# Mamba2 scan and ELU feed-forward on one core: whole-half decays with their sums on GpSimd, low words on ScalarE, and an earlier last weight piece

## The chip, the cores and the metric

The kernel runs on one core of a Trainium2 chip. The core has five engines that each work through their own queue in order: PE (TensorE, matrix products), DVE (VectorE), ACT (ScalarE), POOL (GpSimd) and SP (SyncE, which here only issues DMAs). An instruction whose inputs or buffers aren't ready holds up what stands behind it on its engine. The metric is the device time of one execution in microseconds (us).

## What is computed

Inputs are `x` (4 batches, 8 heads, 768 tokens, 32 wide), decays `a`, and `B` and `C` (16 wide). First a chunked scan, then a feed-forward layer on the 3072 rows that the scan gives:

```python
cum = np.cumsum(log_a, axis=-1)                       # within a chunk of 32
L = np.exp(cum[:, :, :, None] - cum[:, :, None, :]) * causal
y_intra = einsum('bhij,bhjd->bhid', einsum('bhin,bhjn->bhij', Cc, Bc) * L, xc)
y_inter = einsum('bhin,bhnd->bhid', Cc, state) * exp(cum)
state = exp(sum(la)) * state + sum_j(Bc * xc * exp(cum[-1] - cum))
...
h = x @ w_in                                          # (3072, 256) by (256, 2048)
g = np.where(h > 0.0, h, np.exp(np.minimum(h, 0.0)) - 1.0)
out = g @ w_out                                       # (2048, 256)
```

The weights arrive as 64-bit floating-point numbers, and the kernel makes 32-bit ones of their words itself.

## The kernel before

The 3072 tokens are 12 blocks (n = 0 to 11) of 256 tokens. The kernel scans in chunks of 64 tokens instead of 32. For a block the scan has these parts: the table of decays `L` (128 x 8 heads x 2 x 64), the scores `C B`, the product of the two (`weigh`, DVE, L550), the sums for the states (`sums`, PE, L571), the states (`states`: DVE at L588, then a masked copy `Sx` on POOL at L593), the products with the start states (`across`, L616) and inside the chunk (`inside`, L634), whose results ACT copies into `yT` (L651). The feed-forward part has a first product (`l1`, L667, later `l1_words`, L787), the ELU (`elu`: two ACT steps, L680 and L687, and one DVE step, L689, which frees the PSUM buffer of the product) and a second product (`l2`, L829).

**Decays of a block.** `spread_cum(n)` (L377) issues two DMAs that spread the running sums of the logarithms over the partitions into `L`. For one head, `decay_of` (L518) runs two exps on ACT over 128x64 (L521), in place, with `bias=ncum[:, u, row:row + 1]`: the exp subtracts the sum at this partition's token while it reads. After every fourth head, two `affine_select` on POOL (L526, 64x512 each) set to zero what lies after the diagonal. `ncum` is made by PE and a DVE step (L369) just ahead of the loop described next.

**Weights.** There are 16 pieces of 128x512 numbers, 0 to 7 of `w_in` and 8 to 15 of `w_out`. For piece `i`, `w_take` (L966) takes a magnitude on ACT (`w_abs`, L196), the low word (`w_low`, on ACT at L205 or on DVE at L209) and the sign on DVE (L223); `w_give` (L972) makes the high word in two DVE steps (L231, L238) and adds the low word on POOL (`w_sum`, L248). PE can use the piece after that sum.

**Order of the work around the change.** The order is written out by hand. A first loop (L1092) has 12 steps s = 0 to 11. Step s does `l1` for one of (1, 0), (1, 1), (1, 2), (0, 4), (1, 3), (0, 5), (1, 4), (0, 6), (1, 5), (0, 7), (1, 6), (1, 7), where (n, i) is block n with piece i; the first eight steps each do one head of the decays of block 2; odd steps take and give one piece of weights (5 to 10); the ELU follows one step behind. After step 7 come `scores(2)` and `sums(2)`; in step 8 `states(2)`; in step 9 half of the decays of block 3; in step 10 `across(2)` and `inside(.., 2)`. A second loop (L1173) has steps j = 0 to 7: `l2(0, j)`, `l1` of block 2 or 3, pieces 11 to 15 in steps 0, 2, 3, 4 and 5, the rest of block 3's decays in step 0, and `decay` of blocks 4 and 5 in `scan_ahead`. In step 4 `words_of_y(2)` (L750) splits the result of the scan into two words: `y1` (one half on ACT, L755, one on DVE, L759, but both on ACT for n = 4) and `y0` (DVE, L762); `both_of_y` (DVE, L772) follows in step 5. `words_of_w` (ACT L736, DVE L737) and `low_of_w` (POOL, `sub`, L845) split pieces of `w_in`.

From j = 8 on, `l1_words(n, m)` makes the first product in three passes of PE: `y1` by the high word, `y0` with the low word `w0`, and `both_y` with `both_w`. Their order is chosen at L786:

```python
for ps, lhs, rhs in passes if n > 2 and m == 0 else passes[2:] + passes[:2]:
```

So the pass with `both_y` comes first except at the first product of the blocks from 4 on. PSUM has seven buffers for all of this and an eighth for the second product; a new product waits for the last reader of the buffer it takes.

Of the kernel before, what the change touches and what calls it, by code (L numbers as in the profile page):

```python
# [14 lines left out]
ALU = mybir.AluOpType  # L15
ACT = mybir.ActivationFunctionType

P = 128
Q = 64
# [13 lines left out]
def kernel(  # L33
# [27 lines left out]
    nc = tc.nc  # L61
    NB, NH, S, D = x.shape
    N = B.shape[-1]
    NG = S // BLK
# [18 lines left out]
    def psum(shape, name):  # L83
        return p_a.tile(shape, F32, tag="a", name=name)
# [7 lines left out]
    for k in range(4):  # L92
        (nc.scalar if k % 2 else nc.sync).dma_start(
            out=la0[BH * k:BH * (k + 1)],
            in_=a.rearrange("b h (c s) -> (b h) c s", s=P)[:, 0:2, :])
# [5 lines left out]
    st = {}  # L101

    def place(n):

        return 2 * (n // (2 * NG)) + n % 2, n // 2 % NG

    def rows_of(n):
        b, g = place(n)
        return slice(NG * NH * b + g, NG * NH * (b + 1), NG)
# [93 lines left out]
    def w_low(i, eng, cols=slice(None)):  # L203
        if eng is nc.scalar:
            eng.activation(  # L205
                pieces[i][0][:, :, cols], w_words(i)[0][:, :, cols], ACT.Identity,
                scale=2.0 ** -51, bias=two)
        else:
            eng.tensor_scalar(  # L209
                out=pieces[i][0], in0=w_words(i)[0], scalar1=2.0 ** -51, scalar2=2.0,  # L210
                op0=ALU.mult, op1=ALU.add)
# [30 lines left out]
    def w_high(i):  # L242
        w_high_a(i)
        w_high_b(i)
# [34 lines left out]
    for v in range(2):  # L279
        nc.gpsimd.affine_select(  # L280
            out=low16[Q * v:Q * v + Q], in_=low16[Q * v:Q * v + Q], pattern=[[1, Q]],
            compare_op=ALU.is_ge, fill=-65536.0, base=0, channel_multiplier=-1)
# [4 lines left out]
        out=hmask, in_=hmask, pattern=[[-N, NH]], compare_op=ALU.is_ge, fill=0.0,  # L287
        base=0, channel_multiplier=1)
    nc.gpsimd.affine_select(
        out=hmask, in_=hmask, pattern=[[N, NH]], compare_op=ALU.is_ge, fill=0.0,  # L290
        base=N - 1, channel_multiplier=-1)
# [7 lines left out]
        out=minus, in0=ident, scalar1=-1.0, scalar2=None, op0=ALU.mult)  # L299
# [213 lines left out]
    def decay(n, q):  # L513

        decay_of(n, 2 * q)
        decay_of(n, 2 * q + 1)

    def decay_of(n, h):  # L518
        L, row = st[n]["L"], rows_of(n).start + NG * h
        for u in range(2):  # L520
            nc.scalar.activation(  # L521
                L[:, h, u], L[:, h, u], ACT.Exp, bias=ncum[:, u, row:row + 1])
        if h % 4 == 3:
            for v in range(2):
                part = L[Q * v:Q * v + Q, h - 3:h + 1]
                nc.gpsimd.affine_select(  # L526
                    out=part, in_=part, pattern=[[0, 4], [0, 2], [1, Q]],
                    compare_op=ALU.is_ge, fill=0.0, base=0, channel_multiplier=-1)

# [218 lines left out]
    def words_of_y(n):  # L750

        y = yT[n // 2].rearrange("p k b u i -> p k (b u i)")
        y1 = conv.tile([P, KC, 2 * BLK], F32R, tag="y1", name="y1", bufs=1)
        y0 = conv.tile([P, KC, 2 * BLK], F32R, tag="y0", name="y0", bufs=1)
        nc.scalar.activation(y1[:, 1], y[:, 1], ACT.Copy, scale=NEAR / WORD)  # L755
        if n == 4:
            nc.scalar.activation(y1[:, 0], y[:, 0], ACT.Copy, scale=NEAR / WORD)
        else:
            nc.vector.tensor_scalar(  # L759
                out=y1[:, 0], in0=y[:, 0], scalar1=NEAR / WORD, scalar2=None, op0=ALU.mult)  # L760
        for k in range(KC):
            nc.vector.scalar_tensor_tensor(  # L762
                out=y0[:, k], in0=y1[:, k].bitcast(F32), scalar=WORD, in1=y[:, k],
                op0=ALU.mult, op1=ALU.subtract)
        y_words[n] = y1, y0
# [11 lines left out]
    def l1_words(n, m, between=None):  # L777

        cols = slice(m % 2 * P, (m % 2 + 1) * P)
        w, w0 = k_words[m // 2]  # L780
        w1, both_w, w0 = w[:, 0, :, cols], w[:, 1, :, cols], w0[:, :, cols]
        y1, y0, both_y = y_words[n]
        high, both = psum([P, 2 * BLK], "ps_h"), psum([P, 2 * BLK], "ps_w")
        passes = [(high, w1, y1), (high, w0, y0), (both, both_w, both_y)]
        for ps, lhs, rhs in passes if n > 2 and m == 0 else passes[2:] + passes[:2]:
            for k in range(KC):  # L786
                nc.tensor.matmul(  # L787
                    out=ps, lhsT=lhs[:, k], rhs=rhs[:, k], start=k == 0 and lhs is not w0,
                    stop=k == KC - 1 and lhs is not w1)
        if between:  # L790
            words_of_y(between)
        e = ffn.tile([P, 2 * BLK], F32, tag="e", name="e", bufs=2)
        nc.scalar.activation(e, both, ACT.Copy, scale=WORD)  # L793
        if late:
            end_words()
        nc.vector.scalar_tensor_tensor(  # L796
            out=high, in0=high, scalar=WORD - 1.0, in1=e, op0=ALU.mult, op1=ALU.add)
        late.append((n, m, high, e))
# [8 lines left out]
    def end_words():  # L807
        n, m, h, e = late.pop(0)
        g_of[n, m] = ffn.tile([P, 2, BLK], F32, tag=f"g{m % 2}", name="g", bufs=12)
        nc.vector.scalar_tensor_tensor(  # L810
            out=g_of[n, m].rearrange("p b i -> p (b i)"), in0=e, scalar=1.0, in1=h,
            op0=ALU.subtract, op1=ALU.max)
        if m % 2 == 0 and (n, m) != (2, 14):
            sub(g_of[n, m][:, 1], g_of[n, m][:, 1], g_of[n, m][:, 0])
# [151 lines left out]
    def w_take(i, low):  # L966

        w_abs(i)
        w_low(i, low)
        w_sign(i)  # L970

    def w_give(i):  # L972

        w_high(i)
        w_sum(i)
# [10 lines left out]
    half = [slice(0, P), slice(P, 2 * P)]  # L986
# [97 lines left out]
    ncum = turned(F[:, 0], "ncum", -1.0, nc.vector)  # L1084
# [3 lines left out]
    w_load(10)  # L1088
    write_flat(2)

    todo = 5
    for s, (n, i) in enumerate((  # L1092
            (1, 0), (1, 1), (1, 2), (0, 4), (1, 3), (0, 5), (1, 4), (0, 6), (1, 5), (0, 7),
            (1, 6), (1, 7))):
        l1(n, i, parts=2 if s < 2 else 1)
        if s < 8:
            decay_of(2, s)
        if s == 7:
            st[0] = kept
            scores(2)  # L1100
            sums(2, 0, pool=p_o, tag="o", parts=(None, last))
            weigh(2, 0)
            weigh(2, 1)
        if s % 2 == 1 and todo < 11:
            w_take(todo, nc.vector)
            w_give(todo)
            w_load(todo + 6)
            todo += 1
        if s in (1, 3):
            load_bc(3, us=(s // 2,))  # L1110
        if s == 9:
            write_flat(0)
        if s == 4:
            scaled(2, nc.gpsimd)
        if s == 5:
            turn(2)
            turn_exp(2)
        if s == 4:
            load_x(3)
            spread_exp(3)  # L1120
        if s == 8:
            weigh(2, 2)
            weigh(2, 3)
            states(0, last)
            st.pop(0)
            states(2)
        if s == 9:
            decay(3, 0)
            decay(3, 1)
        if s == 10:  # L1130
            spread_cum(4)
            inside(across(2), 2)
        if len(lag) > 1:
            elu()
# [38 lines left out]
    for j in range(2 * DIRECT):  # L1173
        n, i = 2 + j // DIRECT, j % DIRECT
        if j < 7:
            l2(0, j)
        piece = todo < len(pieces) and j != 1
        if j == 0:
            elu()
        if piece:  # L1180
            w_take(todo, nc.vector)
        l1(n, i)
        if j == 7:
            l2(0, j)
        if j == 0:
            scaled(3, nc.gpsimd)
            turn(3)
            elu()
            turn_exp(3)
        if piece:  # L1190
            w_give(todo)
            todo += 1
        while lag:
            elu()
        if j == 0:
            decay(3, 2)
            decay(3, 3)
        if j == 1:
            scores(3)
            sums(3)  # L1200
            for q in range(4):
                weigh(3, q)
        if j == 2:
            states(3)
        if j == 3:
            inside(across(3), 3)
        if j == 4:
            words_of_y(2)
        if j == 4:
            words_of_w(4)  # L1210
        if j == 5:
            low_of_w(4)
        if j == 5:
            both_of_y(2)
        scan_ahead(j)
        if j == 3:
            s_out[:] = weight_sums()
        if j == 6:
            differences(0, 4)
        if j == 7:  # L1220
            words_of_w(5)
# [81 lines left out]
    for n in range(4, NP, 2):  # L1303
        m = n + 2 if n + 2 < NP else None
# [45 lines left out]
    n = NP - 2  # L1350
# [34 lines left out]
```

## Time and profile before

| | |
|---|---|
| median of three runs | 350.15 us (349.95 to 351.11) |
| the profiled execution | 350.85 us |
| its span, first to last instruction | 349.1 us |
| PE busy | 339.9 us, 97% |
| DVE busy | 259.0 us, 74% |
| ACT busy | 234.7 us, 67% |
| POOL busy | 216.8 us, 62% |
| granted clock of PE | 1.000 |

The profile is of one execution, which took 350.85 us; the 1.75 us beside its span lie ahead of the first instruction or behind the last. A timeline row gives the start, the time, the engine, the line, the operation with its output and inputs, how many were merged, and in brackets the idle time before it with what ended it. The time of a merged row reaches to the end of its last instruction, and neighbours overlap a little, so the step from one start to the next is what a queue pays. Within a waits row stand the total, the number of times and the longest.

### The profile page before, as it was taken

Reading aid. Unit: us, or ns where it says so; the run is one execution under the profiler, and the core shown is the slowest. Engines: PE = TensorE matmul, PEld = TensorE weight load, DVE = VectorE, ACT = ScalarE, POOL = GpSimd, SP = SyncE. Lnnn points to the kernel's source line nnn. Section 1 sums busy time; section 2 is a strip of 40 time slices with the busy share of each in tenths; the row PEclk is TensorE's granted clock in tenths of the full one; section 3 lists DMA queues with packets and bytes.
Section 4 is the critical chain, followed back from the end, with each engine's and each line's share of the span. In section 5 each row is a group of like instructions: output and inputs, shape, how many; then the busy total and the mean of one; then the engine's idle time right before and its main releaser. Section 6 shows DMA issues by size and latency. Waiting matters only on the chain.

```text
span 349.1 us, 9873 instructions
## 1 busy us (share of the span) xinstructions
PE 339.9 (97%) x3878; PEld 297.5 (85%) x3878; DVE 259.0 (74%) x515; ACT 234.7 (67%) x537; POOL 216.8 (62%) x338
## 2 busy tenths in 40 slices
PE   7889999998999999999999999999999999999996
PEld 4669888887777889988999988989988999999996
DVE  4898988879997889875878775888675756665232
ACT  5689989597748889657699447699557466565000
POOL 5554554566999599984196764196854174455760
PEclk9999999999999999999999999999999999999999
DMA  8878988470261331070431070320000100001002
GB/s 145 220 220 180 303 175 252 95 132 31 66 126 23 91 62 32 8 151 15 106 62 32 8 160 4 99 40 2 2 0 5 62 0 3 0 0 56 9 0 62
DMA packets 72727, 26.49 MB, mean 76 GB/s; under 512 B 57768, under 2 KB 67560, under 8 KB 72680
## 3 DMA queue, kind: packets, MB, share of 16 engines
q1 hardware_dynamic: 70360, 25.60, 31.4%
q8 instruction: 30, 0.49, 0.6%
q10 hardware_dynamic: 2320, 0.26, 0.5%
q14 instruction: 17, 0.14, 0.1%
HBM read 22.51 MB, written 3.34 MB: 74 GB/s over the span
## 4 chain that ended last, share of the span: by engine, by line
PE 87%; DVE 3%; DMA 3%; SPq 3%; ACT 1%; issue 1%; POOL 1%; DVEq 0%; POOLq 0%; ACTq 0%
PE ps_o L904 36%; PE ps_h L787 18%; PE ps_h L667 11%; PE ps_w L787 9%; PE ps_o L829 6%; PE ps_y L634 3%; DMA w<-in_moe_w_in_dram 2%; PE ps_g L541 2%; PE ps_y L616 2%; PE ps_st L571 1%; DMA bc<-in_C_dram 1%; DVE y_both L772 1%; SPq L116 1%; SPq L178 1%; PE ps_o L890 1%
## 5 line engine op out<-in xcount | busy, mean ns | idle before, releaser
L904 PEld LDWEIGHTS ps_o<-w_out,g 128*128 128x128 f32 x640 | 78.5, 191 | 3.5
L904 PE MATMUL ps_o<-w_out,g 128*128 128x128 f32 x640 | 80.1, 275 | 0.0
L802 ACT ACTIVATE e<-ps_h 128x512 f32<-128x512 f32 x72 | 43.0, 598 | 50.5 <-DVE ps_h L796 50.5
L810 DVE SCALAR_TENSOR_TENSOR g<-e,ps_h 128x512 f32<-128x512 f32 x72 | 49.3, 685 | 31.1 <-ACT e L803 30.8
L845 POOL TENSOR_TENSOR g<-g 128x256 f32<-128x256 f32 x36 | 26.5, 737 | 57.3 <-DVE g L810 57.2
L796 DVE SCALAR_TENSOR_TENSOR ps_h<-ps_h,e 128x512 f32<-128x512 f32 x72 | 50.1, 695 | 13.1 <-ACT e L793 10.0
L793 ACT ACTIVATE e<-ps_w 128x512 f32<-128x512 f32 x72 | 42.3, 587 | 15.0 <-PE ps_w L787 14.9
L787 PE MATMUL ps_w<-y_both,w_words 128*128 128x512 f32 x144 | 51.5, 437 | 0.1
L667 PE MATMUL ps_h<-yT,w_in 128*128 128x256 f32 (+1 forms) x208 | 45.2, 368 | 2.5 <-POOL w_in L248 1.6
L803 ACT ACTIVATE e<-e 128x512 f32<-128x512 f32 x72 | 45.5, 632 | 2.3
L787 PE MATMUL ps_h<-y,w_words 128*128 128x512 f32 x144 | 45.6, 398 | 0.0
L787 PE MATMUL ps_h<-y,w 128*128 128x512 f32 x144 | 45.0, 392 | 0.2 <-POOL w L845 0.2
L667 PEld LDWEIGHTS ps_h<-yT,w_in 128*128 128x128 f32 x208 | 36.3, 190 | 8.4 <-POOL w_in L248 3.6
L521 ACT ACTIVATE L<-L,ncum 128x64 f32<-128x64 f32 x160 | 42.2, 336 | 0.2
L904 PE MATMUL ps_o<-w_sum,g 128*128 128x128 f32 x304 | 38.6, 276 | 0.0
L904 PEld LDWEIGHTS ps_o<-w_sum,g 128*128 128x128 f32 x304 | 37.0, 192 | 1.3
L526 POOL TENSOR_SCALAR_AFFINE_SELECT L<-L 64x512 f32<-64x512 f32 x40 | 29.2, 731 | 9.6 <-ACT L L521 7.5
L787 PEld LDWEIGHTS ps_h<-y,w 128*128 128x128 f32 x144 | 27.0, 188 | 7.1 <-POOL w L845 0.7
L787 PEld LDWEIGHTS ps_h<-y,w_words 128*128 128x128 f32 x144 | 26.7, 188 | 6.2 <-issue 0.5
L829 PE MATMUL ps_o<-w_out,g 128*128 128x256 f32 x128 | 30.9, 384 | 1.0 <-POOL w_out L248 1.0
L845 POOL TENSOR_TENSOR g<-t,g 128x256 f32<-128x256 f32 x40 | 28.1, 734 | 5.8 <-PE ps_o L904 5.7
L845 POOL TENSOR_TENSOR g<-g,t 128x256 f32<-128x256 f32 x40 | 28.7, 747 | 0.2
(133 smaller groups left out, 535.9 us busy)
## 6 DMA issues: line engine op xcount, KB each, us to landing
L<-flat SPq DMA_DIRECT2D x20, 256.0 KB
w<-in_moe_w_out_dram SPq DMA_DIRECT2D x8, 512.0 KB
w<-in_moe_w_in_dram SPq DMA_DIRECT2D x7, 512.0 KB
xr<-in_x_dram SPq DMA_DIRECT2D x24, 128.0 KB
out_dram<-c_sum SPq DMA_DIRECT2D x9, 256.0 KB
bc<-in_B_dram SPq DMA_DIRECT2D x24, 64.0 KB
bc<-in_C_dram SPq DMA_DIRECT2D x22, 64.0 KB
ec<-flat_exp SPq DMA_DIRECT2D x10, 128.0 KB
```

Of the source, the lines that this page charges most:

```text
L521: nc.scalar.activation(L[:, h, u], L[:, h, u], ACT.Exp, bias=ncum[:, u, row:row + 1])
L526: nc.gpsimd.affine_select(out=part, in_=part, pattern=[[0, 4], [0, 2], [1, Q]], compare_op=ALU.is_ge, fill=0.0, base=0, channel_multiplier=-1)
L667: nc.tensor.matmul(out=ps[:, j, toks], lhsT=w_in[i][:, k, j * P:(j + 1) * P], rhs=yT[n // 2][:, k, n % 2].rearrange("p u i -> p (u i)")[:, ...
L787: nc.tensor.matmul(out=ps, lhsT=lhs[:, k], rhs=rhs[:, k], start=k == 0 and lhs is not w0, stop=k == KC - 1 and lhs is not w1)
L793: nc.scalar.activation(e, both, ACT.Copy, scale=WORD)
L796: nc.vector.scalar_tensor_tensor(out=high, in0=high, scalar=WORD - 1.0, in1=e, op0=ALU.mult, op1=ALU.add)
L802: nc.scalar.activation(e, high, ACT.Relu, scale=-1.0)
L803: nc.scalar.activation(e, e, ACT.Exp, scale=-1.0)
L810: nc.vector.scalar_tensor_tensor(out=g_of[n, m].rearrange("p b i -> p (b i)"), in0=e, scalar=1.0, in1=h, op0=ALU.subtract, op1=ALU.max)
L829: nc.tensor.matmul(out=o_of[n][:, ts], lhsT=g_of[n, j][:, m % 2, ts * P:(ts + 1) * P], rhs=w_out[:, m], start=(m == 0 and ts == 0), stop=( ...
L845: nc.gpsimd.tensor_tensor(out=out, in0=in0, in1=in1, op=ALU.subtract)
L904: nc.tensor.matmul(out=ps[:, ts], lhsT=b[:, ts * P:(ts + 1) * P], rhs=a[:, i], start=(i == chunk[0] and ts == 0), stop=(i == chunk[-1]), s ...
```

## The change

Blocks 2 and 3 no longer do their decays head by head. A half of a block (four heads, 128x512) takes three instructions in three consecutive steps: `from_token` adds `ncum` to the spread sums on POOL, `wide_exp` does one exp on ACT without a bias, and `mask` does the two `affine_select` on POOL. For block 2 the adds are issued ahead of s = 0 and in s = 1, the exps in s = 0 and 2, the masks in s = 1 and 3. For block 3 these are s = 7 and 9, 8 and 10, 9 and 11; the part of block 3 that lay in j = 0 is gone. The other blocks keep `decay_of`.

The low words of pieces 5 to 15 are made by ACT and not by DVE. `words_of_y(2)` makes both halves of `y1` on ACT, as it did for n = 4. Piece 15 is taken and given at j = 4, ahead of `words_of_y(2)`, and not at j = 5. `l1_words(2, 8)`, the first of its kind, takes the pass with `both_y` last.

On ACT 32 exps of 128x64 go, and 4 exps of 128x512, 11 low words and one half of `y1` come. On DVE 11 low words and that half of `y1` go. On POOL 4 adds come. PE's instructions and the DMAs stay as many as they were and in their order, but for the passes of that one product.

```diff
+    def from_token(n, half, eng=nc.gpsimd):
+        part = st[n]["L"][:, 4 * half:4 * half + 4]
+        first_row = rows_of(n).start + 4 * NG * half
+        eng.tensor_tensor(
+            out=part, in0=part,
+            in1=ncum[:, :, first_row:first_row + 4 * NG:NG].rearrange(
+                "p u h -> p h u").unsqueeze(3).to_broadcast([P, 4, 2, Q]), op=ALU.add)
+    def wide_exp(n, half):
+        part = st[n]["L"][:, 4 * half:4 * half + 4]
+        nc.scalar.activation(part, part, ACT.Exp)
+    def mask(n, half):
+        for v in range(2):
+            part = st[n]["L"][Q * v:Q * v + Q, 4 * half:4 * half + 4]
+            nc.gpsimd.affine_select(
+                out=part, in_=part, pattern=[[0, 4], [0, 2], [1, Q]],
+                compare_op=ALU.is_ge, fill=0.0, base=0, channel_multiplier=-1)
...
-        if n == 4:
+        if n < 6:
             nc.scalar.activation(y1[:, 0], y[:, 0], ACT.Copy, scale=NEAR / WORD)
...
-        for ps, lhs, rhs in passes if n > 2 and m == 0 else passes[2:] + passes[:2]:
+        for ps, lhs, rhs in passes if m == (8 if n == 2 else 0) else passes[2:] + passes[:2]:
...
+    def step(s):
+        for n, at in ((2, -1), (3, 7)):
+            for half in range(2):
+                if s == at + 2 * half + 2:
+                    mask(n, half)
+                if s == at + 2 * half:
+                    from_token(n, half)
+                if s == at + 2 * half + 1:
+                    wide_exp(n, half)
+    step(-1)
...
         l1(n, i, parts=2 if s < 2 else 1)
-        if s < 8:
-            decay_of(2, s)
+        step(s)
...
-            w_take(todo, nc.vector)
+            w_take(todo, nc.scalar)
...
-        if s == 9:
-            decay(3, 0)
-            decay(3, 1)
...
         if piece:
-            w_take(todo, nc.vector)
+            w_take(todo, nc.scalar)
...
-        if j == 0:
-            decay(3, 2)
-            decay(3, 3)
+        if j == 4:
+            w_take(todo, nc.scalar)
+            w_give(todo)
+            todo += 1
```

In the changed kernel `from_token` is at L522, `wide_exp` at L529 and `mask` at L534; what follows them lies 16 lines later than before, and what follows the loops a little more.

More of the change, by code (lines that the diff above doesn't have):

```diff
@@ L523, in decay_of @@
         if h % 4 == 3:
[L524 to L528, printed above, removed]
+            mask(n, h // 4)
     def scores(*ns):
```

## The prediction

> **What bounds the kernel now.** I read the busy shares first (PE 97% of the span), then the table by stretches, then PE's waits, then the timelines of the engines. The table's columns are the stretch, its length, the busy time (instructions) of PE, weight loads, DVE, ACT and POOL, the granted clock, the DMA share and GB/s.
>
> ```profile
> 27.50:42.25 14.75, 14.75 (x84) 13.08 (x85) 13.45 (x26) 13.84 (x35) 7.29 (x7) 1.00 0.99 245
> 42.25:50.16 7.91, 7.90 (x193) 6.49 (x192) 7.27 (x20) 6.77 (x19) 4.06 (x8) 1.00 0.90 200
> 69.00:81.50 12.50, 12.50 (x79) 10.63 (x63) 10.56 (x18) 12.31 (x39) 6.09 (x7) 1.00 0.55 104
> 81.50:118.00 36.50, 34.86 (x434) 27.48 (x434) 32.53 (x57) 24.23 (x50) 31.80 (x52) 1.00 0.29 63
> ```
>
> From 27.5 to 81.5 us, all of the first loop and most of the second, PE has no gap and the clock is full. Nothing the change does to ACT or DVE can be won there; anything that arrives late is lost one for one. But ACT is busy 13.84 of 14.75 us beside it: it has 0.9 us to spare and POOL has half its time. What PE loses near the change are these two waits:
>
> ```profile
> PE ps_o L829 <- POOL w_out L248: 1.0, 1, 1.0
> PE ps_h L787 <- POOL w L845: 0.2, 1, 0.2
> ```
>
> The first is `l2(0, 7)` at 81.52 us, waiting for piece 15 of the weights (the sum at 81.22 on POOL); the second is `l1_words(2, 10)` at 92.0, waiting for `low_of_w(5)`.
>
> **What comes out.** Piece 15 moves from step j = 5 to j = 4, ahead of `words_of_y(2)`: its last word is then ready several us before PE asks, so the 1.02 us goes. The late `y_both` (DVE, 81.59 to 84.17) is the next thing on that path; `l1_words(2, 8)` now takes it last, 0.9 us after its first product, so it costs nothing. POOL, busy 31.80 of 36.50 us from 81.5 on, begins its `low_of_w(4)` without the w_out sum just ahead of it, so the 0.19 us goes too. **Gain: 1.02 + 0.19 = 1.21 us.** On DVE 11 low words (step 0.34 to 0.8 us each) and one copy of y go, which no PE wait named.
>
> **What goes onto ACT.** A low word on ACT steps 0.66 us (19.63 to 20.29, L205). A half block of decays loses eight exps of 0.24 (2.00 us for x8) for one exp of 128x512, which steps 0.53 (31.03 to 31.56, L687). Up to the elu of (0, 5), ACT loses seven heads of 0.48 (3.36) and gains two wide exps and three low words (1.06 + 1.98 = 3.04). That is even. What is not even is where ACT waits.
>
> **First chain, s = 0 to 7.** The rows of before:
>
> ```profile
> 28.10 0.63 ACT L687 ACTIVATE e<-e 128x512 f32<-128x512 f32 x1
> 28.87 1.06 ACT L521 ACTIVATE L<-L,ncum 128x64 f32<-128x64 f32 x4
> ...
> 41.21 0.63 ACT L687 ACTIVATE e<-e 128x512 f32<-128x512 f32 x1
> ```
> ```profile
> 28.72 1.27 POOL L248 TENSOR_TENSOR w_in<-mag,w_in 128x512 uint32<-128x512 uint32 x1 [2.82 <-DVE mag L238]
> 33.83 1.47 POOL L526 TENSOR_SCALAR_AFFINE_SELECT L<-L 64x512 f32<-64x512 f32 x2 [0.77 <-DMA xr<-in_x_dram]
> ```
> ```profile
> 42.87 0.66 PE L571 MATMUL ps_st<-xr,sc 64*32 64x64 f32 x40
> ```
>
> ACT starts its decays at 28.87, as soon as `ncum` is there, because the bias is inside the exp. In the changed kernel the exp waits for an add on POOL, and in POOL's queue that add stands behind the sum of piece 4, which starts at 28.72 and can't start sooner. ACT works in order: behind the wide exp stand the magnitudes and low word of piece 5 and the elus of the whole loop.
>
> The add (128x512, two inputs, one repeated along the row) is not in the trace. Nearest rows: L248 on 128x512, 1.27 to 1.28 us; L408 on 128x256 with a repeated input, 0.64 to 0.83. Scaling L408's pair by the 128x64 row (0.29) gives 1.10 for the fast one, doubling the slow one 1.66. I take 1.28 (same size, and twice 0.64), with 1.10 and 1.66 as ends. A cost below zero is excluded: the add is extra work on POOL and ACT stands behind it.
>
> - POOL: first add 29.99 to 31.27. ACT idles from 28.73 to 31.27, 2.5 us.
> - ACT: wide exp to 31.80 (its end 31.90), magnitude 32.37, low word 33.03, elu 34.18.
> - POOL: masks of the first half 31.90 to 33.29 (1.39 for two), second add to 34.57, sum of piece 5 to 35.84 (PE wants it at 36.53: in time).
> - ACT idles 34.18 to 34.57, then wide exp 35.10, elu 36.25, piece 6 (0.57 + 0.66) 37.48, two elus 39.78, piece 7 41.01, copy 41.28, elu 42.43, elu of (0, 5) 43.58.
>
> In before that elu ended its step at 41.74: it is 1.84 us later. The built program shows who waits for it: the first of `sums(2)` takes the PSUM buffer that its DVE step frees. DVE ran that step 41.94 to 42.63 and PE started `sums(2)` at 42.87. Now it ends at 44.47, so **PE starts `sums(2)` 1.6 us late** (the scores just ahead wait inside this time).
>
> **Second chain, s = 8 to 11.** The program puts the first mask and the second add of block 3 (s = 9) on POOL behind the five `Sx` of `states(2)`, the wide exp (s = 10) behind that add, and the six copies of `yT` behind that exp on ACT. PE's (1, 7) and then (2, 0) wait for those copies; (1, 7) for the first, whose buffer it takes.
>
> ```profile
> 46.72 1.54 DVE L588 SCALAR_TENSOR_TENSOR S_new<-S_new,ec,ps_st 128x64 f32<-128x64 f32 x5
> 47.07 1.56 POOL L593 TENSOR_TENSOR Sx<-S_new,hmask 128x64 f32<-128x64 f32 x5
> 49.85 1.66 ACT L651 COPY yT<-ps_y 128x128 f32<-128x128 f32 x6 [1.02 <-PE ps_y L634]
> 50.16 1.99 PE L667 MATMUL ps_h<-yT,w_in 128*128 128x256 f32 x8
> ```
>
> DVE, from the end of the step above (44.39): two weighs 0.67, sign 0.34, two high words 1.06, g 0.60, two weighs 0.66, five states 1.46: 49.18, whose last result stands at 49.26. POOL: last `Sx` 49.63, masks 51.02, add 52.30. ACT: wide exp 52.30, next step 52.83, first copy out at 53.11. PE by itself would reach (1, 7) at 44.47 + 7.29 (42.87 to 50.16 in before) = 51.76: **another 1.35 us.** In before the copies came only after PE's own products, so this wait is new. From here PE is 53.11 - 50.16 = **2.95 us late**.
>
> After that ACT has room: the eight decays of j = 0 (2.00 us) are gone and its idle 2.89 us before 64.27 remains. Piece 15 and both halves of y1 on ACT (about 1.8 us more in j = 4) fall into its idle 2.53 us before 84.57, so I cost them at nothing; if that cover were gone, the copy of `ob` would hold `l2(1, 0)`, with 0.3 us to spare as I walk it.
>
> **Sum.** 2.95 - 1.21 = +1.74 us. The profiled execution took 350.85 us (span 349.1 and 1.75 around it), 0.70 above the median of the three runs; on it 352.6, on the median **351.9**. An add of 1.10 moves three adds in series, 0.54 less (351.4); of 1.66, 1.14 more (353.0).
>
> **Two pages.** The Trainium skill, GPSIMD Engine Reference, section Performance versus the Vector engine, measures a two-input add of 2048 elements at 4497 ns; a quarter of that is an estimate of 1.12 us, by which the sum would be 0.5 lower; L248's 1.28 on this very size is used. The same page, Engine selection, speaks against the change itself: two-input elementwise work belongs on VectorE.
>
> **Rivals.** A change under 0.3% (1.05 us) can't be told from none.
> - *ScalarE's relief wins.* Per half block ACT is freed of 8 x 0.24 - 0.53 = 1.4 us; if the adds come early enough that ACT never waits, both chains vanish, 1.21 is gained: 348.9. It decides at an add of under about 0.45 us for the first chain, and a POOL queue without the `Sx` for the second. For it: POOL is idle half the stretch. Against: that idle time (2.82 us) lies before 28.72, when `ncum` isn't there. The Trainium skill, VectorE: DVE Perf Modes, section The TRN2 errata, has the rule behind this rival: a wide operation pays the fixed cost once, many small ones each time. The rows agree (0.63 against 2.00 us). 0.10.
> - *Only one chain costs.* PE's buffers are freed in time in one of the places: +1.6 - 1.2, 350.5. For it: the first chain has only the 0.24 us of margin as measure, the second hangs on the order of four engines. 0.15.
> - *POOL becomes the bound.* Masks took up to 2.00 us a pair (76.34) where DVE was beside them. With 2.0 us per add, three in series give +2.2, and the sum of piece 5 comes after PE's 36.53: 354.0. 0.13.
> - *Forecast*, both chains: 351.3 to 353.1. 0.62.
>
> The range takes the forecast, the one-chain case and the lower half of the last: 350.2 to 354.0. Slower by over 0.3% (above 351.2): nearly all of 0.62, all 0.13 and a little of the 0.15: 0.76. Faster (below 349.1): 0.10. Within: 0.14.
>
> **What would show it.** Right: ACT idle some 2.5 us at 28.7, released by POOL at L522; PE waits of about 1.6 us ending at the scores and sums near 44 and 1.3 us at (1, 7) near 52, released by ACT's copy; no wait for w_out near 84. Wrong: an add under 0.5 us, ACT not idle at 28.7, PE gapless through 55 us; or a w_out wait still there.

## The result and the profile after

Beside the kernel before, on one chip, the changed kernel took 353.22 us (median of 8 runs, 352.40 to 356.25) and the kernel before 350.63 us (8 runs, 349.95 to 351.11): a ratio of 1.0079, 95% interval 1.0050 to 1.0108. The change costs 2.6 us. The profiled execution took 352.86 us with a span of 350.7 (before: 350.85 and 349.1).

First three rows of the table by stretches, which answer to the first three of before (same columns), and then the second of them in slices of 2 us:

```profile
27.20:42.00 14.80, 14.79 (x84) 13.01 (x84) 9.61 (x20) 11.46 (x21) 9.67 (x10) 1.00 0.95 238
42.00:53.40 11.40, 10.21 (x194) 8.00 (x193) 10.93 (x23) 8.94 (x17) 7.89 (x12) 0.85 0.86 193
69.00:84.45 15.45, 15.45 (x163) 13.16 (x162) 11.78 (x22) 15.25 (x43) 9.07 (x12) 1.00 0.51 90
```
```profile
42.00:44.00 2.00, 1.12 (x28) 0.77 (x32) 1.75 (x5) 1.97 (x4) 1.79 (x2) 1.00 1.05 333
44.00:46.00 2.00, 1.69 (x63) 1.21 (x48) 1.97 (x6) 1.97 (x4) 0.49 (x1) 0.71 0.87 117
46.00:48.00 2.00, 2.00 (x6) 1.63 (x5) 2.00 (x5) 1.97 (x5) 1.26 (x1) 0.50 0.92 261
48.00:50.00 2.00, 2.00 (x10) 1.72 (x9) 1.86 (x7) 1.97 (x4) 1.79 (x7) 0.94 0.52 58
```

ACT is busy 11.46 of 14.80 us where it was busy 13.84 of 14.75. That is not relief: of the 3.34 us in which it is idle, 3.15 are the two waits shown next (2.49 and 0.66), and the work that they hold up comes later. The second stretch, which held PE full at clock 1.00, now has PE idle for 1.2 us, and after that gap the granted clock is 0.71, 0.50 and 0.94 in three slices. The prediction has no such term.

ACT, and below it POOL, at the first chain:

```profile
27.81 0.63 ACT L703 ACTIVATE e<-e 128x512 f32<-128x512 f32 x1
30.93 0.63 ACT L529 ACTIVATE L<-L 128x512 f32<-128x512 f32 x1 [2.49 <-POOL L L522]
34.63 0.63 ACT L529 ACTIVATE L<-L 128x512 f32<-128x512 f32 x1 [0.66 <-POOL L L522]
```
```profile
28.43 1.27 POOL L248 TENSOR_TENSOR w_in<-mag,w_in 128x512 uint32<-128x512 uint32 x1 [2.83 <-DVE mag L238]
29.66 1.24 POOL L522 TENSOR_TENSOR L<-L,ncum 128x512 f32<-128x512 f32 x1
31.64 1.50 POOL L534 TENSOR_SCALAR_AFFINE_SELECT L<-L 64x512 f32<-64x512 f32 x2 [0.74 <-ACT L L529]
33.22 1.37 POOL L522 TENSOR_TENSOR L<-L,ncum 128x512 f32<-128x512 f32 x1
```

The brackets of the two wide exps are the first chain: ACT stood for 2.49 us until the add on POOL was done, and POOL itself went from the sum of piece 4 straight into that add. What it does to PE, in PE's timeline and in DVE's, and then the second chain in ACT's:

```profile
42.81 1.51 PE L557 MATMUL ps_g<-ctm,bct 32*64 32x128 f32 x32 [0.78 <-DVE ctm L436]
44.63 0.79 PE L587 MATMUL ps_st<-xr,sc 64*32 64x64 f32 x40 [0.31 <-POOL L L522]
45.35 6.86 PE L683 MATMUL ps_h<-yT,w_in 128*128 128x256 f32 x24
52.14 0.49 PE L632 MATMUL ps_y<-bct,Sx 32*64 32x64 f32 x32
```
```profile
41.98 0.68 DVE L436 TENSOR_TENSOR ctm<-ps_tc,hmask 128x512 f32<-128x512 f32 x1
43.85 0.69 DVE L705 SCALAR_TENSOR_TENSOR g<-e,ps_h 128x512 f32<-128x512 f32 x1 [0.26 <-ACT e L703]
```
```profile
52.32 0.63 ACT L529 ACTIVATE L<-L 128x512 f32<-128x512 f32 x1 [2.19 <-POOL L L522]
53.08 1.66 ACT L667 COPY yT<-ps_y 128x128 f32<-128x128 f32 x6
```

The scores wait for `ctm`, which stands in DVE's queue behind ELU steps that waited for ACT; in before it was made at 40.10 us. The bracket of `sums(2)` names POOL's add, but these products use nothing of it: e2 below has no add at that place and the same gap (0.32 us). What ends just ahead, at 44.54 us, is DVE's `g` of (0, 5), as the prediction says.

From here on, places are counted from PE's start on the transposes of `ncum` (L364: at 26.93 us in before, 26.65 in the changed kernel), because that start itself lay between 25.9 and 29.0 us in the profiles of this study, apart from e10, which moves it. `sums(2)` starts 17.98 us after it instead of 15.94: 2.04 us late. The 24 products behind it take 6.86 us instead of 5.45, at the lowered clock. In before:

```profile
43.54 5.45 PE L667 MATMUL ps_h<-yT,w_in 128*128 128x256 f32 x24
```

ACT stands a second time, 2.19 us, but its copies of `yT` start at 53.08, 0.52 us after PE's products inside the chunk, as in before (49.85 after 49.33): PE, slowed by the clock, came no sooner. (1, 7) starts at 53.40, 3.52 us late.

PE's waits:

```profile
PE ps_g L557 <- DVE ctm L436: 0.8, 1, 0.8
PE ps_h L683 <- DVE M L566: 0.5, 1, 0.5
PE ps_st L587 <- POOL L L522: 0.3, 1, 0.3
PE ps_h L803 <- POOL w L861: 0.2, 1, 0.2
```

The wait of 1.0 us for piece 15 is gone. The one of 0.2 us for `low_of_w(5)` is not. A wait for `yT` is not in the list at all, because the lowered clock filled it. `l2(0, 7)` starts 57.80 us after the transposes instead of 55.61 (+2.19), the first product of the last phase (L920) +2.50.

### The profile page after: what moved, and what is told of

Read it like the earlier page. It is cut to its first block, busy times and chain, and to the rows that moved or that the text cites. A ratio compares the mean times of both kernels' runs of the same rounds, so it can differ in the third digit from the quotient of the medians.

```text
span 350.7 us, 9851 instructions
## 1 busy us (share of the span) xinstructions
PE 343.3 (98%) x3878; PEld 299.9 (86%) x3878; DVE 253.7 (72%) x503; ACT 236.7 (68%) x521; POOL 221.8 (63%) x342
## 3 DMA queue, kind: packets, MB, share of 16 engines
HBM read 22.51 MB, written 3.34 MB: 74 GB/s over the span
## 4 chain that ended last, share of the span: by engine, by line
PE 77%; ACT 7%; POOL 6%; DVE 2%; SPq 2%; issue 2%; DMA 2%; POOLq 0%; ACTq 0%; DVEq 0%
PE ps_o L920 36%; PE ps_h L803 18%; PE ps_w L803 9%; PE ps_h L683 5%; PE ps_o L845 4%; PE ps_y L650 2%; POOL L L534 2%; DMA w<-in_moe_w_in_dram 2%; PE ps_st L587 1%; PE ps_y L632 1%; ACT e L696 1%; PE ps_g L557 1%; POOL L L522 1%; ACT mag L196 1%; ACT L L541 1%
## 5 line engine op out<-in xcount | busy, mean ns | idle before, releaser
L920 PEld LDWEIGHTS ps_o<-w_out,g 128*128 128x128 f32 x640 | 78.5, 191 | 3.4
L920 PE MATMUL ps_o<-w_out,g 128*128 128x128 f32 x640 | 80.1, 275 | 0.0
L683 PE MATMUL ps_h<-yT,w_in 128*128 128x256 f32 (+1 forms) x208 | 46.5, 375 | 1.6 <-POOL w_in L248 1.1
L683 PEld LDWEIGHTS ps_h<-yT,w_in 128*128 128x128 f32 x208 | 37.3, 195 | 7.7 <-POOL w_in L248 2.3
L920 PE MATMUL ps_o<-w_sum,g 128*128 128x128 f32 x304 | 38.6, 276 | 0.0
L920 PEld LDWEIGHTS ps_o<-w_sum,g 128*128 128x128 f32 x304 | 37.0, 192 | 1.3
L534 POOL TENSOR_SCALAR_AFFINE_SELECT L<-L 64x512 f32<-64x512 f32 x40 | 30.5, 764 | 8.5 <-ACT L L541 6.4
L541 ACT ACTIVATE L<-L,ncum 128x64 f32<-128x64 f32 x128 | 33.7, 337 | 0.0
L861 POOL TENSOR_TENSOR g<-g,t 128x256 f32<-128x256 f32 x40 | 28.7, 748 | 0.2
```

The lines of the kernel that those rows point to most:

```text
L534: nc.gpsimd.affine_select(out=part, in_=part, pattern=[[0, 4], [0, 2], [1, Q]], compare_op=ALU.is_ge, fill=0.0, base=0, channel_multiplier=-1)
L541: nc.scalar.activation(L[:, h, u], L[:, h, u], ACT.Exp, bias=ncum[:, u, row:row + 1])
L683: nc.tensor.matmul(out=ps[:, j, toks], lhsT=w_in[i][:, k, j * P:(j + 1) * P], rhs=yT[n // 2][:, k, n % 2].rearrange("p u i -> p (u i)")[:, ...
L861: nc.gpsimd.tensor_tensor(out=out, in0=in0, in1=in1, op=ALU.subtract)
L920: nc.tensor.matmul(out=ps[:, ts], lhsT=b[:, ts * P:(ts + 1) * P], rhs=a[:, i], start=(i == chunk[0] and ts == 0), stop=(i == chunk[-1]), s ...
```

## The experiments

Two theories: **the queue theory**, that the loss is ACT standing twice behind adds which stand in POOL's queue behind other work, and **the load theory**, that the work moved (low words on ACT, adds and masks on POOL) is itself too much. Twelve runs, each timed beside before (e4 and e12 are one kernel, e9 is before itself). "Late" is the start of `sums(2)` after the `ncum` transposes, against before's 15.94 us (of e10, which moves these transposes, after those of `eb`, against 15.72).

| kernel | median us (runs) | ratio to before, interval | late us |
|---|---|---|---|
| e1_heads2 | 356.03 (5) | 1.0156, 1.0131 to 1.0182 | 1.20 |
| e2_heads3 | 353.33 (8) | 1.0082, 1.0053 to 1.0112 | 2.08 |
| e3_heads23 | 351.68 (12) | 1.0031, 1.0017 to 1.0045 | 1.21 |
| e4_piece15 | 350.45 (12) | 0.9998, 0.9984 to 1.0012 | 0.00 |
| e5_dve_adds | 350.27 (12) | 1.0008, 0.9995 to 1.0021 | 0.63 |
| e6_no_add | 349.25 (12) | 0.9975, 0.9956 to 0.9994 | 0.00 |
| e7_add_twice | 358.15 (5) | 1.0229, 1.0214 to 1.0244 | 4.29 |
| e8_adds_first | 350.25 (12) | 1.0006, 0.9991 to 1.0020 | 0.40 |
| e9_before_again | 350.17 (10) | 0.9997, 0.9981 to 1.0014 | 0.00 |
| e10_ncum_early | 350.64 (12) | 1.0001, 0.9983 to 1.0019 | 0.22 |
| e11_block2_first | 352.06 (5) | 1.0048, 1.0031 to 1.0064 | 0.41 |
| e12_piece15_again | 350.25 (11) | 0.9991, 0.9978 to 1.0004 | 0.00 |

Before had medians of 350.47, 350.24 and 350.40 us in the three batches (e1 to e4, e5 to e8, e9 to e12).

### One part at a time

**e1_heads2**: block two by heads again, the rest as changed.

```
-        for n, at in ((2, -1), (3, 7)):
+        for n, at in ((3, 7),):
...
-        step(s)
+        if s < 8:
+            decay_of(2, s)
+        step(s)
```

> Block 2's decays head by head again (no add on POOL ahead of them), everything else as changed. Queue theory (ACT stands behind the adds at two places): ACT no longer idles at 28.7, but seven heads (3.36 us) and three low words (1.98) stand together on it, so sums(2) is still about 1.1 us late instead of 2.0; the second chain (copies of yT behind the wide exp of block 3) stays. About 351.5 to 352.3. Rival (the low words on ACT are the whole loss): as slow as the changed kernel, 353.2, with PE's gap at the scores and sums as long as there.

Its `sums(2)` is 1.2 us late instead of 2.0, yet it is the slower kernel, 356.03. PE's row at (1, 7), and the granted clock behind it:

```profile
53.65 3.15 PE L683 MATMUL ps_h<-yT,w_in 128*128 128x256 f32 x8 [1.94 <-ACT yT L667]
```
```profile
52.00:54.00 2.00, 0.35 (x2) 0.33 (x3) 1.92 (x2) 1.16 (x4) 1.31 (x2) 1.00 0.96 327
54.00:56.00 2.00, 2.00 (x7) 1.60 (x6) 0.00 (x0) 1.90 (x6) 1.94 (x3) 0.58 1.00 365
56.00:58.00 2.00, 2.00 (x6) 1.59 (x6) 1.66 (x4) 1.97 (x4) 0.08 (x1) 0.57 1.12 270
```

The second chain now shows as an open wait of 1.94 us, and the clock falls behind it to 0.58 and 0.57: eight products take 3.15 us where they took 1.99. The 1.2 us and the wait were expected; the time is some 4 us above the expectation. The clock is one part of that: PE is 3.7 us late at (1, 7) and 5.4 us late sixteen products further on, so it costs 1.7 us here. The second chain is also longer than in e11 below, where (1, 7) is 1.95 us late: beside POOL's mask and add (43.49 to 46.07 us) two rows of DVE (L223 and L231) took 0.85 and 1.27 us, in e11, with POOL idle, 0.42 each; the states and the second add come later by that. The clock alone can't be the reason, for the one run at a mean clock of 1.000 took 354.99 us; what is left stays open.

**e2_heads3**: block three by heads again (its `decay` calls back at s = 9 and j = 0), block two wide.

```
-        for n, at in ((2, -1), (3, 7)):
+        for n, at in ((2, -1),):
...
+        if s == 9:
+            decay(3, 0)
+            decay(3, 1)
...
+        if j == 0:
+            decay(3, 2)
+            decay(3, 3)
```

> Block 3's decays head by head again, block 2 wide, the rest as changed. Queue theory: the first chain stays (2 us at the scores and sums near 44) and ACT's copies of yT no longer wait for POOL near 52. If the lowered clock behind that gap (0.5 for some 3 us in the profile of the changed kernel, about 1.4 us of PE work) was only hidden by the second chain, it shows now and the time stays near 353; if the clock holds, 351.5 to 352. Rival (low words): no change, 353.2, whatever the clock.

The first chain is there unchanged (2.08 us late) and no wait at (1, 7). The runs fall in two groups: four at a mean clock of 1.0 took 351.32 to 352.59 us, four at 0.994 to 0.995 took 354.07 to 355.41. So this kernel costs some 1.7 us where the clock holds and some 2.5 more where it falls behind the gap at the scores and sums. At full clock it is about 1 us under the changed kernel, which has the second chain too. The median says little of such a pair.

**e3_heads23**: both blocks by heads (both edits above); the low words on ACT, the early piece 15, `y1` and the order of passes stay.

> Both blocks head by head as before the change; low words on ACT, the early piece 15, y1 on ACT and the order of the passes stay. Queue theory: sums(2) 1.1 us late from ACT's load, no second chain, w_out wait gone: 350.0 to 350.8, about the time before. Rival (low words on ACT are the loss): 352.5 or more.

351.68, 1.2 us above before, with `sums(2)` 1.21 us late. It differs from e4 below only in the engine of the low words, and e4 takes 350.45: low words on ACT without the relief of the wide exps cost 1.2 us. (A wait of 0.8 us at the sums of a later block, put down to POOL's L730, also appears in its profile, which the changed kernel has not.) The time is 0.9 us over the expectation and under the rival's 352.5; the expectation had counted on the gain at piece 15, which does not show in e4's median either.

**e4_piece15** and **e12_piece15_again**, one kernel twice: e3 with the low words back on DVE (`w_take(todo, nc.vector)`), that is before with piece 15 a step earlier, `y1` on ACT and `y_both` last.

> The kernel before with only piece 15 at j = 4, y1 of block 2 on ACT and y_both last in l1_words(2, 8); low words on DVE, decays head by head. Queue theory: the 1.02 us wait for w_out goes and perhaps 0.2 more: 349.4 to 349.7. Rival (the gain is given back, because y0 and y_both come later on DVE behind piece 15): 350.5, with a new PE wait at l1_words(2, 8).

> The same kernel as e4_piece15, a second time, for its tail: in the first profile the last product ended 1.0 us sooner relative to the ncum transposes than in before, but 6.0 us instead of 5.2 lay between the start of the last product and the end of the span. If the long tail was that one execution's, it is 4.8 to 5.2 us here and the median of these runs is 349.3 to 349.9; if the kernel itself gives the gain back, the tail is again near 6 us and the median again within 0.3 us of before's.

Both profiles lose the wait for piece 15: `l2(0, 7)` comes 1.18 and 1.03 us sooner, the first product of the last phase 1.16 and 1.02. And no median shows it: 350.45 against 350.47 and 350.25 against 350.40. From the start of the last 16 products to the end of the span it takes 6.0 and 5.8 us in these two profiles, 5.2 in before, 4.9 in the changed kernel. The last store, in before and in e4:

```profile
346.31 0.35 SPq L896 DMA_DIRECT2D out_dram<-c_sum  x1
```
```profile
345.17 0.35 SPq L912 DMA_DIRECT2D out_dram<-c_sum  x1
```

PE's work is done sooner and the tail takes back 0.6 to 0.8 of it. Why the tail is longer (the last store is issued as before, and the span ends 3.3 and 3.1 us after that issue instead of 2.4) stays open.

**e9_before_again**, the kernel before a second time:

> The kernel before, unchanged, a second time. If its wait of 1.02 us for piece 15 of the weights at l2(0, 7) belongs to the kernel, the profile shows it again (0.9 to 1.1 us) and the time is the same as before's within 0.2%. If it belonged to that one execution, the wait is gone or under 0.4 us.

The wait belongs to the kernel:

```profile
PE ps_h L667 <- DVE g L689: 1.4, 1, 1.4
PE ps_g L541 <- ACT bct L420: 1.1, 1, 1.1
PE ps_o L829 <- POOL w_out L248: 1.0, 1, 1.0
```

This profiled execution was that kernel's longest (352.30 us), for another reason: the first two waits, at 20 to 24 us, are not in the first profile of the same kernel, and the clock was 0.66 and 0.50 in the two slices behind them. These gaps near the start came in one of the two profiled executions; with them the transposes of `ncum` were 2 us late.

### The adds

**e6_no_add**: the changed kernel without its adds; the decays of blocks two and three leave out the subtraction of a token's own sum.

```
-                if s == at + 2 * half:
-                    from_token(n, half)
```

> The changed kernel without the adds; it leaves out the subtraction of a token's own sum from the decays of blocks two and three. Queue theory: ACT's wide exp waits for nothing on POOL, no idle at 28.7 us, sums(2) at its old place after ncum (within 0.3 us), no wait at (1, 7), 349.3 to 350.5. Rival (low words on ScalarE, or masks on POOL, are the loss): 351.5 or more, sums(2) still over 1 us late.

```profile
27.57 0.61 ACT L529 ACTIVATE L<-L 128x512 f32<-128x512 f32 x1
```
```profile
41.80 0.66 PE L587 MATMUL ps_st<-xr,sc 64*32 64x64 f32 x40
```

The first wide exp starts with no idle time before it. `sums(2)` is at its old place to 0.01 us (the transposes started at 25.86 us), there is no wait at (1, 7), and the time is 349.25 us. Low words on ACT, masks on POOL a step behind, wide exps: all of that is in this kernel, and together it costs nothing. The load theory falls here for all but the adds themselves, which e8 brings back.

**e7_add_twice**: each add done twice; the token's sum is subtracted twice.

```
                     from_token(n, half)
+                    from_token(n, half)
```

> Each add of the changed kernel done twice; the token's sum is subtracted twice in blocks two and three. Queue theory: the first chain holds two adds in series ahead of the elu of (0, 5), so sums(2) starts about 2.4 us later still (about 20.4 us after ncum) and block three's chain about another 1 to 2.4: 355 to 357.5. Rival (the adds lie beside other work): under 354.

ACT's three waits grow from 2.49, 0.66 and 2.19 us to 3.63, 1.80 and 4.02:

```profile
31.86 0.63 ACT L529 ACTIVATE L<-L 128x512 f32<-128x512 f32 x1 [3.63 <-POOL L L522]
36.67 0.63 ACT L529 ACTIVATE L<-L 128x512 f32<-128x512 f32 x1 [1.80 <-POOL L L522]
```

`sums(2)` comes 2.25 us later still: two more adds in series (2.38 and 2.50 us for each pair). PE also waits 1.71 us at 37.91 us for the sum of piece 5, which stands behind the adds; ACT's second exp starts 10.24 us after the transposes instead of 7.98, 2.26 later, so ACT's chain still sets `sums(2)`. The median, 358.15, is 7.9 us above before (the changed kernel: 2.6), again with the clock down to 0.50 behind the gap, and a little over what was expected.

**e5_dve_adds**: the adds on DVE.

```
-    def from_token(n, half, eng=nc.gpsimd):
+    def from_token(n, half, eng=nc.vector):
```

> The four adds of the changed kernel on DVE in place of POOL, at the same places of the program. Queue theory (the loss is ACT waiting for adds that stand behind other work in POOL's queue): the add is then shorter (DVE's two-input rows of half that width take 0.42 us, so about 0.7) and stands only behind DVE's g of (0, 3) at 28.5 us; ACT idles under 1 us at 28.7 instead of 2.5, sums(2) starts within 0.8 us of its place in the kernel before (17.98 us after ncum in the changed kernel, 15.94 before), the wait at (1, 7) is gone or under 0.5 us, and the time is 350.0 to 351.2. Rival (the low words on ScalarE are the loss, whatever engine adds): sums(2) stays 1.2 to 2 us late and the time stays above 351.7.

350.27 us, the time of before. ACT still idles 1.84 us ahead of the first exp, more than expected, since DVE does both adds in one go (1.52 us) behind `eb` and a `g`; but the second one then waits for nothing, and the chain is 1.4 us shorter.

**e8_adds_first**: the adds stay on POOL. Both adds of a block are issued together, block two's ahead of the sum of piece 4, block three's at s = 7 ahead of the `Sx` and the masks.

```
     w_high_b(4)
-    w_sum(4)
     ncum = turned(F[:, 0], "ncum", -1.0, nc.vector)
...
-                if s == at + 2 * half:
+                if s == at:
                     from_token(n, half)
...
     step(-1)
+    w_sum(4)
```

> The changed kernel with its adds on POOL as they are, but both adds of a block issued together, block two's ahead of the sum of weight piece 4, block three's (both at s = 7) ahead of the Sx of states(2) and of its masks. The same work on each engine, another order on POOL. Queue theory: the first add begins at ncum's arrival (about 26.9 us) and ends before ACT is free at 28.7; no idle there, sums(2) within 0.4 us of its old place after ncum, no wait for yT at (1, 7) beyond 0.3 us, no drop of the granted clock at 44 to 50 us, 349.3 to 350.6. Rival (the added work itself, on ScalarE or on POOL, is the loss): sums(2) over 1 us late and 351.7 or more.

The same instructions on every engine in another order on POOL: 350.25 us, by the ratios to before 2.6 us under the changed kernel.

```profile
30.11 0.63 ACT L529 ACTIVATE L<-L 128x512 f32<-128x512 f32 x1 [1.28 <-POOL L L522]
```

Half of the first idle time is left, for DVE's `ncum` step starts only at 28.59 us here, behind copies and a high word. There is no wait at (1, 7), the clock is 1.00 throughout. So the loss against before is the place of the adds in POOL's queue, as the queue theory says. Of the 1.0 us between e6 and e8 this does not say how much is the idle time that is left and how much the adds' own work.

**e11_block2_first**: block two's adds as in e8, block three's as changed.

```
-                if s == at + 2 * half:
+                if s == (at if n == 2 else at + 2 * half):
```

> The changed kernel with block two's adds issued first, as in e8_adds_first, and block three's left where the change put them. Theory (two separate chains): sums(2) within 0.6 us of its old place, but PE waits 1 to 2 us for ScalarE's yT at (1, 7), as in e1_heads2, and the granted clock falls behind that wait: 351.5 to 354.5. Rival (the second chain is a consequence of the first): no such wait, 350 to 350.6 as e8_adds_first.

352.06: between the two. The second chain by itself, in ACT's and PE's timelines:

```profile
50.76 0.63 ACT L529 ACTIVATE L<-L 128x512 f32<-128x512 f32 x1 [2.84 <-POOL L L522]
```
```profile
51.60 1.99 PE L683 MATMUL ps_h<-yT,w_in 128*128 128x256 f32 x8 [1.46 <-ACT yT L667]
```

The wait is 1.46 us, and the clock stayed at 1.0 in all five runs, where a fall was expected. The two chains are separate: the ratio falls by 0.0031 when the first is mended (1.1 us) and by another 0.0042 (1.5 us) with the second.

**e10_ncum_early**: e8, with `ncum` turned ahead of `l1(0, 3)`.

```
     weigh(1, 3)
+    ncum = turned(F[:, 0], "ncum", -1.0, nc.vector)
     l1(0, 3)
...
-    ncum = turned(F[:, 0], "ncum", -1.0, nc.vector)
```

> e8_adds_first, and ncum turned ahead of l1(0, 3) instead of behind across(1): DVE's ncum step comes some 2 us sooner, so both adds of block two lie in POOL's idle time ahead of the sum of piece 4. Queue theory: the first add begins near 26.5 us, ACT has no idle time at 28.7 released by POOL, sums(2) is at its old place after the eb transposes (within 0.2 us), the time comes near e6_no_add's 349.25: 349.0 to 350.0, faster than before by 0.1 to 0.4%. Rival (what is left in e8 against e6 is the adds' own work): 350.2, as e8_adds_first.

A miss. The first add does start at 26.57 us and ACT idles no more at 28.7, but the median is 350.64. In this profile POOL then stands at block three's adds:

```profile
43.67 2.53 POOL L522 TENSOR_TENSOR L<-L,ncum 128x512 f32<-128x512 f32 x2 [2.45 <-DMA L<-flat]
```

At s = 7 their input is only just arriving; the add waited 2.45 us for that transfer, and ACT's wide exp 1.35 us for the add. PE's two open waits behind it are 0.2 us each, but counted from the `eb` transposes PE is 0.22 us late at `sums(2)` and 1.45 us at the end of `across(2)`, where e8 is 0.33 us late. The early transposes cost something too: PE waits 0.7 us at L364 for the PSUM buffer that a `g` on DVE frees. A place early enough for ACT is in this execution too early for the load. e8 has block three's adds at the same place without that wait, with the transfers issued at 32.25 us and not at 33.37; and this profiled execution took 352.11 us, 1.5 above its median. Whether the wait belongs to the kernel is not shown, so what is left between e6 and e8 stays open. No version that computes the whole of the reference beat the kernel before by more than its interval.

## Why the prediction was right, and where it was off

- **First chain.** Right in mechanism and nearly in size: ACT idle 2.49 us (2.5 said), the second wait 0.66 (0.39), the adds 1.24, 1.37, 1.05 and 1.10 us (1.28 taken), `sums(2)` 2.04 us late (1.6). e6 and e8 show that it is the adds' place in POOL's queue, e7 that two adds stand in series in it.
- **"That is even"** of ACT's work: shown from both ends. With the low words on ACT alone `sums(2)` is 1.2 us late (e3), with the wide exps beside them 0.0 (e6).
- **Second chain.** 1.35 us said, 1.46 measured where it stands alone (e11). In the changed kernel's own profile the sign that was named, a PE wait of 1.3 us at (1, 7), is not there: the lowered clock, which the prediction did not have, brings PE there no sooner than the copies. (1, 7) is 3.52 us late, 2.95 said; that the size is near is luck in this execution, where the clock's 1.4 us (6.86 instead of 5.45) stand in the place of the chain's. The runs show no difference between the two cases: three with a mean clock of 0.995 have a median of 353.21 us, the five others 353.22.
- **The gain of 1.02 us** at `l2(0, 7)`: the wait went, as said. In the changed kernel PE does win it: 3.4 us late ahead of `l2(0, 7)`, 2.2 at it. But its worth was taken at face value: by itself (e4, e12) it moves no median, and in the two profiles a longer tail takes back most.
- **The gain of 0.19 us** failed. The step said that `low_of_w(4)` would begin sooner without the sum ahead of it, and `low_of_w(5)` with it. But `low_of_w(4)` began 57.99 us after the transposes instead of 55.51 and so no sooner against PE, which is 2.2 us late there: masks now stand ahead of it. And POOL does the masks of block four between the two in both kernels (1.72 us for two before, 2.33 after). The wait is 0.2 us in every profile but that of e3.
- **The size.** 351.9 said, 353.2 measured. 0.48 of the difference is the base: the median of before was 350.15 in three runs and 350.63 beside the changed kernel. Further: the chains 0.57 more, the 0.19, and 0.27 outside the span, which the prediction had left at before's value (2.07 us on the mean of the changed kernel's runs against 1.80 in before's). Some 0.3 came back at `across(3)`; a like amount was lost between 84 and 120 us. Of that, 0.15 is at `l2(1, 0)`, which waits for the copy of `ob` (87.11 to 87.67 us, PE at 87.72): ACT's idle 2.53 us before that copy is used up, and the 0.3 us to spare were not there. These sizes come partly from medians and partly from one profile and do not add up exactly. Within the profiled pair the account closes: PE's last 16 products start 2.17 us later after the transposes, the transposes 0.28 sooner, and the tail is 0.3 shorter, which is the 1.6 us between the spans.
- **The rivals.** *ScalarE's relief wins* needed adds that ACT never waits for; e6 is that case and gains 1.0 us instead of the 1.2 that was said. *Only one chain costs* is e11, 1.7 us above before where 350.5, 0.35 above its base, was said, and e2, 1.7 above at full clock. *POOL becomes the bound* did not come in the changed kernel: no sum of piece 5 was late. It comes in e7, with 2.4 to 2.5 us of adds in each place: PE waits 1.71 us for that sum.

The rule of the Trainium skill (GPSIMD Engine Reference, section Engine selection) that two-input elementwise work belongs on VectorE was named against the change. e5 bears it out in part: on DVE an add took 0.68 to 1.01 us instead of 1.05 to 1.37 and the loss was gone. But e8 got the same time from POOL by order alone.

## What to carry to other kernels

A bias inside an activation is an operand that adds no wait on a further queue (the first decay started at 28.87 us in before, at 30.93 in the changed kernel): taking it out to make one wide instruction of many small ones saves work on one engine and hangs that in-order engine on another. Before counting the saving, find what stands ahead of the new producer in its queue and what stands behind the new consumer in its own; if the pair is kept, issue the producer as soon as its inputs have landed, and no sooner. A wait that a profile shows on the busiest engine is worth its length only if nothing behind it, down to the last store, takes it back.

## What the hardware showed that was not expected

**The clock fell behind gaps of one to two microseconds.** In the changed kernel PE's rows show 1.2 us of idle time in all between 42 and 44.7 us. The scores among them take 1.51 us instead of 0.69 at full clock, so more was lost: from the end of the product ahead (42.03) to `sums(2)` (44.63) lie 2.60 us, in before 0.55 (42.32 to 42.87). The slices behind have a granted clock of 0.71, 0.50 and 0.94. With half rate as the lower step, that is 1.16 + 2.00 + 0.24 = 3.4 us at half rate (a slice of 2 us at 0.71 holds 2 x 0.29 x 2). The same sum gives 3.4 us in e1 (0.58, 0.57), and in the repeat of before (0.66, 0.50, 0.99). So such a stretch costs 1.7 us, as PE's places in e1 show, or less where PE would have waited anyway (e2's two groups of runs lie 2.5 us apart, which is more; why stays open). The Trainium skill, TensorE: Matmul & The Clock Gate, section What's actually happening, has the clock at full or half rate, judged in free-running windows of 3413 ns: the length agrees. It asks for an idle window of some 3.4 us before the clock falls; here 2.0 us lost out of 2.6, with scores between two gaps, were enough, and the measurement decides. That a window's phase decides would fit that three of the changed kernel's eight runs had a mean clock of 0.995 and the others 0.999 or 1.0, and that e11's gap of 1.46 us never brought the clock down; what exactly triggers it is not shown.

**Single runs spread by more than the parts of the change.** Runs of e8, all at a mean clock of 0.999 or 1.000, still spread from 349.3 to 352.1 us, those of e5 from 349.6 to 352.0: so a part of 1 us is read from medians or from places within a profile.
